# Due times of the first batch's value loads, sums of squares and scale in an attention and feed-forward kernel

## The chip, the cores and the metric

The kernel runs as one program on one NeuronCore of a Trainium2 chip. Its five engines are named as in the profile: PE (matrix products), DVE (vector), ACT (activations), POOL and SP, the last of which here only issues transfers. The metric is device time in microseconds (us) of one execution; lower is better. A time before is the median of three executions.

## The reference, cut to what matters

Four batches of 576 tokens and 8 heads of width 64 pass through causal attention with a decay, then through two gated feed-forward blocks of width 512.

```
scores = scale * q @ k.T + (cum[:, None] - cum[None, :])   # cum: running sum of log f, causal mask
attn   = softmax(scores)
x      = attn @ v                                          # per head, heads joined to 512
h = relu(x @ w_in);  u, vv = halves(h);  vn = layernorm(vv)
x = (u * (w_spatial @ vn + b)) @ w_out
x = sigmoid(xr @ w_r) * (relu(xk @ w_k)**2 @ w_v)          # xk, xr: mixes of x and x shifted by a token
```

## The kernel before

Attention is worked in 16 pairs of heads (`p`), 32 heads in all (`g`); batch `b` is pairs 4b to 4b+3. For each pair the kernel loads q and k, squares and sums them to choose a power of two as their scale (`qksq`, `qkscale`), splits them into a high and a low half (`qkhi`, `qklo`), turns them around by a transposing transfer (`qklo` issues it), copies parts of the result into second tiles (`kaux`, `qaux`), computes scores (`score`, L302) and row maxima (`rowmax`, L311 on DVE), and sends the maxima through memory back into a tile (`mrow`). Only then come the transposed scores (`scoreT`, L335), the exponential (L339), and the product with the values (`pv`, L357). Meanwhile the first feed-forward weight is loaded in eight blocks (`wload`, L90), converted (`wconv`), summed (`wscale`) and split (`wsplit`, L440 on ACT and L441 on DVE).

The values of batch 0 are loaded by `vload` in five chunks `c` of two transfers each, all on SP's queue: ten transfers, eight of 128 KB and the two of the last chunk of 64 KB. `vsq` squares each chunk on ACT and sums it into a column of `va`. `vscale` adds the columns up with two small products on PE and turns the sum into a scale by six short DVE instructions (L234, L78, L79, L81, L85, L238). The scale is first read by `recip` of pair 0, due at 2.4; the values are first read by `pv` of head 0, due at 1.0.

```python
    for e in range(2):                                     # vload
        self.nc.sync.dma_start(t[:tn, c, :, 128 * e:128 * e + 64], src[e::2, t0:t0 + tn]...)
    self.sumsq(self.va[:, c:c + 1], t, self.junka...)      # vsq, L66 on ACT
```

**The order.** Each step is entered with a due time, in units of a head, and a priority; `run` sorts by due time, then priority, and emits the steps in that order. The due times that matter here, from the table `P` and the loops (pair `p` adds 2p): the transposing transfers of pair 0 are issued at -4.25 (k) and -3.95 (q), its copies at -3.6 and -3.5; the values of batch 0 are loaded at -3.2, squared at -3.0 to -1.8, and scaled at -1.2; pair 1 is transposed at -2.25 and -1.95 and copied at -1.6 and -1.5; pair 3's k and q are loaded at -2.0 and -1.7; pair 2 is squared at -1.6 and -1.5 and its scale follows at -1.2; `wsplit` of the first four weight blocks stands at -1.4 to -0.5; pair 4's load is at 0.0 and weight block 4's at 0.15.

**The list behind the order.** The emitted order is not the order on the chip. The program is built with `schedule_with_timeline_sim=True` (L869): the framework walks through the emitted program on a timeline of its own and, whenever an engine's queue is free there, appends the earliest emitted instruction that is ready. So a step emitted later goes ahead where an earlier one still waits. Instructions that pass through `pin` (L56) stay behind the instruction emitted before them on the same engine; `wconv` and `wsplit` use it. On the chip each queue then runs as written.

Of the kernel before, what the change touches and what calls it, by code (L numbers as in the profile page):

```python
# [30 lines left out]
P = dict(load=-8.0, sq=-5.6, ss=-5.2, sc=-5.0, hik=-4.6, lok=-4.25, hiq=-4.2, loq=-3.95, aux=-3.6,  # L31
         s=-2.4, m=-0.65, t=0.0, pv=1.0, out=1.35, rc=1.4, nr=1.9, xs=2.2, xl=2.4, mlp=2.7, mlplen=7.0, vload=-5.0, vsq=-3.0,
         w1=-3.8, w0=1.0, wsp=4.6)
# [6 lines left out]
class K:  # L40
# [561 lines left out]
    def add(self, t, prio, fn, *args):  # L602
        self.steps.append((t, prio, len(self.steps), fn, args))
# [7 lines left out]
    def plan_attention(self):  # L611
        add, G = self.add, self.B * self.H
        for p in range(G // 2):
            T = 2.0 * p
            if p > 1:
                add(T + P["load"], 9, self.load, p, "k")
                add(T + P["load"] + 0.3, 9, self.load, p, "q")
            for i, nm in enumerate("kq"):
                add(T + P["sq"] + 0.1 * i, 2, self.qksq, p, nm)
            add(T + P["ss"], 2, self.qkscale, p)  # L620
            add(T + P["hik"], 2, self.qkhi, p, "k", "act")
            add(T - 4.2, 2, self.crow, p)
            add(T + P["lok"], 2, self.qklo, p, "k")
            add(T + P["hiq"], 2, self.qkhi, p, "q", "dve")
            add(T + P["loq"], 2, self.qklo, p, "q")
            add(T + P["aux"], 2, self.kaux, p)
            add(T + P["aux"] + 0.1, 2, self.qaux, p)
            for h in range(2):
                for u in range(4):
                    add(T + P["s"] + h + 0.22 * u, 4, self.score, 2 * p + h, u)  # L630
                    add(T + P["s"] + h + 0.22 * u + 0.05, 1, self.rowmax, 2 * p + h, u)
            add(T + P["m"], 0, self.mrow, p)
        for g in range(G):
            for u in range(4):
                add(g + P["t"] + 0.22 * u, 0, self.scoreT, g, u)
            for c, u in ((0, 0), (1, 1), (2, 2), (3, 2), (4, 3)):
                add(g + P["t"] + 0.22 * u + 0.06, 1, self.causal, g, c)
            for hf in range(2):
                add(g + P["pv"] + 0.3 * hf, 5, self.pv, g, hf)
            add(g + P["out"], 1, self.head, g)  # L640
            if g % 2:
                add(g + P["rc"], 1, self.recip, g // 2)
                add(g + P["nr"], 2, self.norm, g // 2)
                add(g + P["xs"], 2, self.xhi, g // 2)
                add(g + P["xl"], 2, self.xlo, g // 2)
        for b in range(self.B):
            for c in range(5):
                add(8 * b + P["vload"] + 0.2 * c if b else -3.2, 9, self.vload, b, c)
                add(8 * b + P["vsq"] + 0.3 * c, 3, self.vsq, b, c)
            add(8 * b + P["vsq"] + 1.8, 3, self.vscale, b)  # L650

# [219 lines left out]
```

## Time and profile before

| | us |
|---|---|
| median of three executions | 751.83 (749.38 to 755.04) |
| the profiled execution | 752.66 |
| its span, first to last instruction | 750.9 |

Busy shares of the span are PE 90%, DVE 57%, ACT 50%, POOL 25%. The span falls into a filling stage of about 60 us in which the first pairs are loaded and prepared, an attention stage to about 444 us in which attention and the first feed-forward block share PE, and a last stage of matrix products. In a row of the timeline the first number is the start in us from the span's first instruction and the second the duration; what stands in brackets at the end is the engine's idle time before it and what ended it. SPq rows are the issuing of transfers on SP's queue, not their landing.

### The profile page before, as it was taken

The numbers are of one execution on the slowest core, as the hardware profiler recorded it, in microseconds if no ns is written. First come the engines' busy times: TensorE is split into PE (matmuls) and PEld (weight loads), VectorE is DVE, ScalarE is ACT, GpSimd is POOL, SyncE is SP. The second block draws the span as 40 slices with busy tenths as digits, with TensorE's granted clock in tenths as the row PEclk, the third lists the DMA queues.
The fourth block names the chain that finished last, engine by engine and source line by source line (L and its number), as shares of the span: only waits on it lengthen the run. The fifth ranks groups of instructions, "written<-read, shape, count | busy, mean of one in ns | idle before, by whom it ended". The sixth has DMA issues, their size and how long they took to land.

```text
span 750.9 us, 11016 instructions
## 1 busy us (share of the span) xinstructions
PE 674.9 (90%) x3718; PEld 499.5 (67%) x3718; DVE 426.8 (57%) x1147; ACT 372.2 (50%) x740; POOL 184.5 (25%) x385
## 2 busy tenths in 40 slices
PE   0377878989998999999997679999999999999997
PEld 0245545647775677666774458788888888888886
DVE  5987786666655656646026879988225512632342
ACT  4626786666426854355505539747225412622431
POOL 7122645555324544445321201000000000000000
PEclk9998968999999999999999899999999999999999
DMA  9997666765655234410025453450100100010010
GB/s 228 203 204 158 168 138 131 147 137 107 126 133 122 56 71 99 97 27 18 18 64 184 146 192 124 140 164 15 42 27 16 57 0 15 1 56 1 1 57 28
DMA packets 130681, 69.78 MB, mean 93 GB/s; under 512 B 114704, under 2 KB 115312, under 8 KB 130624
## 3 DMA queue, kind: packets, MB, share of 16 engines
q1 hardware_dynamic: 128032, 67.89, 37.1%
q10 hardware_dynamic: 2592, 1.19, 0.7%
q8 instruction: 29, 0.48, 0.3%
q14 instruction: 28, 0.23, 0.1%
HBM read 42.06 MB, written 9.79 MB: 69 GB/s over the span
## 4 chain that ended last, share of the span: by engine, by line
PE 60%; DMA 16%; DVE 10%; POOL 5%; issue 3%; ACT 3%; SPq 1%; DVEq 0%; ACTq 0%; POOLq 0%
PE m L715 40%; PE o L357 7%; DMA sr<-rd 3%; POOL x L388 3%; PE m L575 3%; PE m1v L504 3%; PE s L302 3%; PE t L335 2%; PE m1u L558 2%; DMA rd<-r 2%; DVE junk L311 2%; DMA r<-rd 2%; DMA wst<-in_moe_w_k_dram 1%; DMA rd<-xo 1%; DMA wst<-in_moe_w_in_dram 1%
## 5 line engine op out<-in xcount | busy, mean ns | idle before, releaser
L357 PE MATMUL o<-e,v 128*128 128x320 f32 (+4 forms) x448 | 114.0, 384 | 5.5 <-POOL e L344 3.7
L715 PE MATMUL m<-xx,moe_w_k 128*128 128x512 f32 (+1 forms) x480 | 107.5, 373 | 0.4 <-ACT x L710 0.4
L715 PE MATMUL m<-moe_w_v,k 128*128 128x512 f32 x432 | 104.8, 391 | 0.0
L339 ACT ACTIVATE e<-t,qa 128x512 f32<-128x512 f32 (+1 forms) x128 | 72.6, 590 | 50.4 <-PE t L335 50.1
L311 DVE CUSTOM_DVE_ANT_0 junk<-s,mask 128x512 bf16<-128x512 f32 (+4 forms) x160 | 75.9, 474 | 37.8 <-PE s L302 32.2
L715 PEld LDWEIGHTS m<-xx,moe_w_k 128*128 128x128 f32 x480 | 84.0, 188 | 18.1 <-ACT x L710 0.9
L357 PEld LDWEIGHTS o<-e,v 128*128 128x128 f32 x448 | 78.5, 199 | 23.7 <-POOL e L344 6.1
L715 PEld LDWEIGHTS m<-moe_w_v,k 128*128 128x128 f32 x432 | 80.7, 188 | 17.7
L344 POOL TENSOR_SCALAR_AFFINE_SELECT e<-e 128x128 f32<-128x128 f32 (+1 forms) x160 | 52.2, 342 | 125.5 <-ACT e L339 123.0
L751 DVE TENSOR_TENSOR tmp<-tmp 128x512 f32<-128x512 f32 (+1 forms) x40 | 25.5, 638 | 88.1 <-ACT tmp L750 87.9
L302 PE MATMUL s<-kT,qT 128*128 128x512 f16 (+2 forms) x192 | 55.8, 299 | 21.6 <-DVE nm L311 13.7
L504 PE MATMUL m1v<-win,xt 128*128 128x512 f16 x240 | 61.5, 397 | 0.0
L388 POOL TENSOR_TENSOR x<-xo,sr 64x576 f32<-64x576 f32 x32 | 47.0, 1469 | 47.6 <-DMA sr<-rd 46.4
L715 PE MATMUL m<-gh,moe_w_out 128*128 128x512 f32 (+1 forms) x240 | 55.1, 380 | 3.5 <-DVE u L578 3.5
L335 PE MATMUL t<-qA,kA 69*128 69x512 f16 (+2 forms) x192 | 51.6, 294 | 7.3 <-DMA qA<-md 6.7
L558 PE MATMUL m1u<-xt,win 128*128 128x288 f16 x384 | 53.6, 286 | 4.5 <-ACT u L560 4.5
L750 ACT ACTIVATE tmp<-m 128x512 f32<-128x512 f32 (+1 forms) x40 | 22.1, 556 | 71.6 <-PE m L715 71.4
L575 PE MATMUL m<-wspT,vn 128*128 128x288 f16 x384 | 54.4, 290 | 3.0 <-DVE u L578 2.3
L302 PE MATMUL s<-kA,qA 67*128 67x512 f16 (+2 forms) x192 | 50.6, 300 | 4.0 <-DMA kA<-kT 3.7
L701 POOL COPY x<-x 128x4 f32<-128x4 f32 x4 | 3.5, 884 | 198.1 <-ACT x L710 198.1
L715 PEld LDWEIGHTS m<-gh,moe_w_out 128*128 128x128 f32 x240 | 43.3, 193 | 13.0 <-DVE u L578 3.8
L335 PE MATMUL t<-qT,kT 128*128 128x512 f16 (+2 forms) x192 | 51.4, 293 | 0.0
(159 smaller groups left out, 1083.8 us busy)
## 6 DMA issues: line engine op xcount, KB each, us to landing
sr<-rd SPq DMA_DIRECT2D x32, 144.0 KB
gd<-u SPq DMA_DIRECT2D x16, 288.0 KB
out_dram<-o SPq DMA_DIRECT2D x18, 256.0 KB
knat<-in_k_dram SPq DMA_DIRECT2D x32, 128.0 KB
v<-in_v_dram SPq DMA_DIRECT2D x32, 128.0 KB
g<-gd SPq DMA_DIRECT2D x16, 256.0 KB
wst<-in_moe_w_k_dram SPq DMA_DIRECT2D x8, 512.0 KB
wst<-in_moe_w_v_dram SPq DMA_DIRECT2D x8, 512.0 KB
```

Source lines behind the costliest of these rows:

```text
L302: self.nc.tensor.matmul(s[:, o:o + n], self.tok(qn, p, h, 128 * ib - 64, 128)[0:r], self.tok(kn, p, h, k0, n)[0:r], start=(j == 0), stop=( ...
L311: self.nc.vector.tensor_tensor_reduce(out=self.junk[r0:, 0:n], in0=self.s[u % 2][r0:, o:o + n], in1=self.mask[r0:, m0:m0 + n], op0=ALU.add ...
L335: self.nc.tensor.matmul(t[:, o:o + n], self.tok(kn, p, h, 128 * c, 128)[0:r], self.tok(qn, p, h, q0, n)[0:r], start=(j == 0), stop=(j == 1))
L339: self.nc.scalar.activation(self.e[g][:, 512 * u:512 * u + n], t[:, 0:n], AF.Exp, scale=self.qa[p][:, 5:6])
L344: self.nc.gpsimd.affine_select(out=e, in_=e, pattern=[[1, n]], compare_op=ALU.is_ge, fill=0.0, base=0, channel_multiplier=-1)
L357: self.nc.tensor.matmul(o[:, 256 + f:256 + q1], v[:, c, h // 2, 64 * (h % 2):64 * (h % 2) + 128], e[:, off:off + q1 - f], start=(c == 0), ...
L388: self.nc.gpsimd.tensor_tensor(self.xp[r], self.xo[h][r], self.sr[r], ALU.mult)
L504: nc.tensor.matmul(self.m1p, xt[:, xs, 128 * j:128 * j + 128], self.win[:, ws, kc, 512:1024], start=(kc == 0 and n == 0), stop=(kc == 3 an ...
L558: self.nc.tensor.matmul(o, self.win[:, ws, kc, fs], self.xt[(4 * b + kc) % 8][:, xs, ts_], start=(kc == 0 and n == 0), stop=(kc == 3 and n ...
L575: nc.tensor.matmul(o, pairs[n][0], pairs[n][1], start=(n == 0), stop=(n == 13))
L715: self.nc.tensor.matmul(out, l, r, start=(first and j == 0), stop=(last and j == len(pairs) - 1))
L751: nc.vector.tensor_tensor(tmp[:, 0:n], tmp[:, 0:n], tmp[:, 0:n], ALU.mult)
```

## The change

The first batch's three kinds of steps get later due times. The ten value loads go from -3.2 to between -1.5 and -0.7, the five squarings from -3.0...-1.8 to -1.2...0.0, the scale from -1.2 to 0.6. Other batches keep theirs. No instruction is added, removed or given another size. In the emitted program the value loads now stand behind pair 1's transposes and copies and behind pair 3's loads, the squarings behind pair 2's, and the scale behind pair 2's and behind the first head's first transposed scores.

```diff
         for b in range(self.B):
+            vsq = 8 * b + P["vsq"] if b else -1.2
             for c in range(5):
-                add(8 * b + P["vload"] + 0.2 * c if b else -3.2, 9, self.vload, b, c)
-                add(8 * b + P["vsq"] + 0.3 * c, 3, self.vsq, b, c)
-            add(8 * b + P["vsq"] + 1.8, 3, self.vscale, b)
+                add(8 * b + P["vload"] + 0.2 * c if b else -1.5, 9, self.vload, b, c)
+                add(vsq + 0.3 * c, 3, self.vsq, b, c)
+            add(vsq + 1.8, 3, self.vscale, b)
```

## Rows read from the trace of the kernel before

**Rows 1.** The page's busy tenths in 40 slices of 18.8 us.
```profile
PE   0377878989998999999997679999999999999997
DMA  9997666765655234410025453450100100010010
```

**Rows 2.** Stretches: length; busy us of PE, PEld, DVE, ACT, POOL; clock; DMA; GB/s.
```profile
0.00:28.00 28.00, 2.10 (x6) 1.22 (x7) 18.48 (x36) 13.03 (x28) 15.37 (x43) 1.00 1.02 225
28.00:41.00 13.00, 7.00 (x30) 4.06 (x31) 12.12 (x47) 8.43 (x19) 1.56 (x1) 1.00 0.99 201
41.00:60.00 19.00, 17.25 (x87) 10.30 (x85) 16.77 (x59) 8.57 (x16) 7.65 (x19) 1.00 0.89 191
60.00:145.00 85.00, 72.19 (x389) 47.35 (x389) 61.60 (x231) 57.38 (x124) 41.32 (x73) 0.84 0.70 146
145.00:200.00 55.00, 51.30 (x343) 34.48 (x342) 36.54 (x119) 34.84 (x76) 26.99 (x57) 0.97 0.58 124
```

**Rows 3.** Chain that ended last, 9 to 62 us: start, us, what.
```profile
21.39 4.66 DMA wst<-in_moe_w_in_dram
...
34.20 0.07 DVE va L234
```

**Rows 4.** Timeline of SP's queue, 13 to 33 us: start, us, transfer issued.
```profile
13.62 3.28 SPq L222 DMA_DIRECT2D v<-in_v_dram  x6
17.03 0.42 SPq L206 DMA_DIRECT2D cumd<-u  x1
17.49 0.43 SPq L222 DMA_DIRECT2D v<-in_v_dram  x1
18.02 1.56 SPq L272 DMA_TRANSPOSE qT<-nq  x1
...
23.38 0.49 SPq L278 DMA_DIRECT2D kA<-kT  x1
23.93 2.02 SPq L222 DMA_DIRECT2D v<-in_v_dram  x3
26.00 1.64 SPq L272 DMA_TRANSPOSE kT<-nk  x1
27.68 1.15 SPq L215 DMA_DIRECT2D knat<-in_k_dram  x2
...
29.54 1.42 SPq L272 DMA_TRANSPOSE qT<-nq  x1
31.01 1.25 SPq L215 DMA_DIRECT2D qnat<-in_q_dram  x2
```

**Rows 5.** Timeline of PE at the first scores.
```profile
28.01 0.96 PE L302 MATMUL s<-kA,qA 67*128 67x512 f16 x2 [3.69 <-DMA kA<-kT]
```

**Rows 6.** Timeline of ACT, 17 to 46 us.
```profile
17.65 0.63 ACT L66 ACTIVATE junka<-v 128x512 bf16<-128x512 f32 x1 [0.45 <-DMA v<-in_v_dram]
...
28.39 0.63 ACT L66 ACTIVATE junka<-v 128x512 bf16<-128x512 f32 x1 [1.67 <-DMA v<-in_v_dram]
...
29.02 0.61 ACT L66 ACTIVATE win<-wf 128x512 f16<-128x512 f32 x1
...
30.37 0.74 ACT L66 ACTIVATE junka<-knat 128x640 bf16<-128x640 f32 x1
...
32.45 1.95 ACT L440 ACTIVATE win<-wf,sw 128x512 f16<-128x512 f32 x3 [0.39 <-DVE sw L81]
...
45.02 0.83 ACT L260 ACTIVATE nk<-knat,qa 128x640 f16<-128x640 f32 x1 [7.07 <-DVE qa L81]
```

**Rows 7.** Timeline of DVE, 26 to 42 us.
```profile
26.07 1.27 DVE L100 TENSOR_SCALAR wst<-wst 128x512 int32<-128x512 int32 x1 [0.33 <-DMA wst<-in_moe_w_in_dram]
...
33.46 0.74 DVE L441 SCALAR_TENSOR_TENSOR win<-wf,sw,win 128x512 f16<-128x512 f32 x1
...
41.09 0.15 DVE L238 TENSOR_SCALAR sv<-sv 128x1 f32<-128x1 f32 x1
41.16 0.17 DVE L318 CAST nmh<-nm 128x10 f16<-128x10 f32 x1
```

## The prediction

> **What bounds the kernel now.** I read the page's slices first: PE is busy for nine tenths or more in most of them, but 0, 3 and 7 tenths in the first three, while DMA stands at nine tenths in just these [rows 1]. So the change falls into the filling stage, the one place where PE is not the bound. Next the busy time by stretch: to 28 us PE works 2.1 us; from 28 to 41 us DVE is busy 12.12 of 13 us and PE only 7.0; from 41 to 60 us PE has 17.25 of 19 [rows 2]. The DMA engines are full to 41 us at 201 to 225 GB/s. Then the chain of waits: a weight block's landing at 26.05 us starts DVE's conversions, and from there the chain runs through DVE almost without a break to about 41 us [rows 3]. Then the four queues that the change touches, each in order of time [rows 4 to 7]. A microsecond saved before 41 us can move the end only if it comes off one of two things: the landing that opens the first scores at 28.01 us [rows 5], or DVE's queue between 28 and 41.16 us, where the last row maximum of pair 0 lets `mrow` start [rows 7].
>
> **The change part by part.**
>
> *The value loads on SP.* The list appends what is ready. In the trace the first six loads are issued in one run from 13.62 us, and `cumd`, which was emitted long before them, only behind that run; the seventh follows at 17.49 us [rows 4]. So the list put them there because nothing emitted earlier was ready. What the new due time lets pass ahead of them is pair 1's transposes and copies and pair 3's loads. The first need pair 1's split halves; pair 3's loads go into pair 0's tiles and need pair 0's halves done, which is also what pair 0's transposes, issued from 18.02 us behind the seventh load, waited for. None was ready, so I expect seven of ten to stay where they are: 0 us. The other three (128 and twice 64 KB, 256 KB) come at 23.93 us, behind pair 0's copy `kA<-kT`. There pair 3's k load is ready (emitted at -2.0, before the values' -1.5), and the two change places: k's three transfers, 288 KB, for 256 KB in front of pair 1's k transpose. At 201 GB/s the 32 KB are 0.16 us, on a transpose whose result the first pair does not read. Then q of pair 3 takes the place that k had, and the three value loads land on q's old place: from 23.93 on, k takes 1.86 us (27.68 to the next row's 29.54), q as long, the two transposes 1.64 and 1.42, 6.8 us together, so they go out at about 31 us [rows 4].
>
> Does anything urgent get faster by that? `kA<-kT` was issued at 23.38 us and ended PE's wait at 28.01 [rows 5]; chunk 3, whose second transfer was issued right behind it, ended ACT's wait at 28.39 [rows 6]. They landed in the order of issue, so taking away the later one gives the earlier one 0. If the engines shared their time among both, 256 KB at 201 GB/s would give up to 1.27 us. I take 0, the order in the rows, and keep -1.27 as a bound. The Trainium skill, DMA: Bandwidth & Descriptors, section Queues, rings and completion order, states that each DMA engine consumes descriptors in ring order though completions need not follow it; by that the gain is 0 too, and the rule speaks against the idea that what is asked for later frees what stands ahead. By equal sharing it would be the 1.27.
>
> *The squarings on ACT.* Five of 0.63 us and five read-outs of the sum. They were fillers: the first waited 0.45 us for its data, the fourth 1.67 [rows 6]. Pair 2's squarings (0.74 us each) now stand earlier in the program and should take the first fillers' places at about 17.2 us; in the trace they ran only at 30.37, behind all the values' [rows 6]. The weight's last squaring at 29.02 us stood behind the fourth filler, which ran from 28.39: at most 0.12 us gained, if I set its input's arrival at about 28.9. Where the fillers go: ACT was idle for 7.07 us before 45.02 [rows 6], so their five places cost 0. If that cover is gone they cost 5 x 0.63 = 3.2 us, but of ACT, which is busy 8.57 of 19 us from 41 to 60 [rows 2].
>
> *The scale.* Two small products on PE: no cost, PE is half idle from 28 to 41 us [rows 2]. Six short DVE instructions now stand inside the DVE-bound stretch; the last runs at 41.09, directly before `mrow`'s first at 41.16 [rows 7], and the chain gives one of them 0.07 us net [rows 3], the spacing of those two rows. Six are 0.4 us. With the squarings of the last two chunks waiting for loads of about 31 us they should pass behind 41.16. Pair 2's five scale instructions go the other way, ahead of 26 us: 5 x 0.07 = 0.35 us out of the stretch, into one where DVE waited 0.33 us for the weight block anyway [rows 7], so they cost 0.02 there. Bounds: 0 if the list puts all eleven back between the row maxima; 11 x 0.15 = 1.65 us if the full duration counts.
>
> **The sum.** 0 (loads) - 0.12 (ACT) - 0.4 - 0.33 (DVE) = -0.85 us. Behind 60 us PE has the say, so a start 0.85 earlier is an end at most 0.85 earlier. The profiled execution took 752.66, so 751.8; it lies 0.83 above the median of 751.83, so against the runs shown I predict **751.0**.
>
> **Rivals.**
>
> *A, the loads do go behind.* If the list did not fill the gap at 13.62 us, seven loads (896 KB at 225 GB/s, 4.0 us) would leave the queue ahead of pair 0's transposes, the weight block would land about 4 us before 26.05 and `kA<-kT` before 28.01. Both of the chain's starts would gain about 4 us: 747.8. For it speaks only the wording of the due times; against it that `cumd`, emitted first, was overtaken by six loads.
>
> *B, a new wait on ACT (slower).* Where the list puts chunk 3's and 4's squarings ahead of the three `wsplit` products at 32.45 us, ACT waits for loads issued at about 31 us. They took 4.46 us before (23.93 to 28.39), so they end at 35.5; the weight's DVE part moves from 33.46 by 3 us, and the row maxima behind it in DVE's queue with it. +3 us against the profiled execution, 755.7; against the median 754.8. It decides from the point at which the list's own timeline lets these loads land before `wsplit`'s scale is ready. For it: the list already misjudged these loads by 1.67 us at 28.39 [rows 6]. Against it: `wsplit` is emitted ahead of them and needs only chunks 0 to 2 by its pins. The Trainium skill, TensorE: Matmul & The Clock Gate, in its table of specifications calls ACT's and DVE's queues strict first in, first out; the row at 28.39, with the weight's squaring behind it, agrees. The same price holds if pair 2's halves, ready sooner, make DVE wait for pair 1's transposes.
>
> *C, the list falls differently later.* Every order behind the first difference can change. From 60 to 145 us PE is idle 12.8 of 85 us (15%), from 145 to 200 us 3.7 of 55 (7%), with clocks of 0.84 and 0.97 [rows 2]. If the first stretch ran with the second's share of idle time it would gain 85 x 0.083 = 7.1 us: 744.7; as much lost is 758.9. Nothing in the rows favours one sign.
>
> **How the numbers follow.** The forecast has 0.50, A 0.10, B 0.18, C 0.12 faster and 0.10 slower. About 1% (7.5 us) is what a measurement of this kernel can tell from no change; forecast, A and B lie inside it, and C reaches its edge on either side. Half of C and a tenth of A and B may pass it, and C's faster side a little more, as DVE loses work there: faster by over 1% 0.12, within 1% 0.77, slower 0.11. The forecast's own range is 749 to 752, from its bounds (-2.9 with sharing and full durations, +0.2 with nothing gained). To leave out no more than 2 in 10 the range must hold A, B and most of C: 744 to 759.
>
> **What would show it.** Right: six value loads still from about 13.6 us and one behind `cumd`; three at about 31 us; pair 2's squarings on ACT before 20 us; `mrow` at 40.3 instead of 41.16. Wrong by A: transposes of pair 0 before any value load, and first scores near 24 us. Wrong by B: an idle gap on ACT ended by `v` ahead of L440. Wrong by C: the first 60 us alike and PE's idle time from 60 to 145 us changed by over 4 us.

## The result and the profile after

The changed kernel takes 755.88 us (median of 20 executions, 750.27 to 760.68) against 751.71 us (20, 747.72 to 755.04) for the kernel before on the same chip: a ratio of 1.0055 with an interval of 1.0035 to 1.0075. It is slower by some 4 us. The profiled execution of the changed kernel is the fastest of its twenty (750.27 us, span 748.6 us, mean granted clock 0.982), so its trace shows the order well, but not where the loss lies. For that a second trace of the same order is used (e1 below, span 761.3 us, clock 0.961). Traces of one order differ from execution to execution; where a reading hangs on one trace, the others of its order are named with it.

SP's queue after, in order of time (start, us, transfer issued); it answers to [rows 4]:

```profile
13.96 3.34 SPq L222 DMA_DIRECT2D v<-in_v_dram  x6
...
17.89 0.43 SPq L222 DMA_DIRECT2D v<-in_v_dram  x1
...
24.52 1.22 SPq L215 DMA_DIRECT2D knat<-in_k_dram  x2
...
33.79 1.97 SPq L222 DMA_DIRECT2D v<-in_v_dram  x3
...
42.02 0.66 SPq L90 DMA_DIRECT2D wst<-in_moe_w_in_dram  x1
...
43.81 0.38 SPq L325 DMA_DIRECT2D md<-mr  x1
...
46.91 0.22 SPq L326 DMA_DIRECT2D qA<-md  x1
```

The same queue before, where [rows 4] end:

```profile
36.75 0.59 SPq L90 DMA_DIRECT2D wst<-in_moe_w_in_dram  x1
...
43.58 0.31 SPq L325 DMA_DIRECT2D md<-mr  x1
...
45.35 0.39 SPq L326 DMA_DIRECT2D qA<-md  x1
```

Seven of the ten value loads still go out at 13.96 and 17.89 us, three at 33.79. New is the row at 42.02: weight block 4 (512 KB), which before went out at 36.75, now stands 1.8 us ahead of the first row-max reload, `md<-mr` and `qA<-md`.

ACT after, in order of time; it answers to [rows 6]. An idle time stands in brackets with what ended it:

```profile
16.83 0.73 ACT L66 ACTIVATE junka<-knat 128x640 bf16<-128x640 f32 x1
...
29.41 0.63 ACT L66 ACTIVATE win<-wf 128x512 f16<-128x512 f32 x1 [2.26 <-DVE wf L105]
...
32.98 1.95 ACT L440 ACTIVATE win<-wf,sw 128x512 f16<-128x512 f32 x3 [2.85 <-DVE sw L81]
...
37.64 0.63 ACT L66 ACTIVATE junka<-v 128x512 bf16<-128x512 f32 x1 [0.55 <-DMA v<-in_v_dram]
```

Pair 2's squarings run at 16.83 us instead of 30.37. The wait ahead of L440 was ended by DVE's scale, not by a value load.

DVE after; it answers to [rows 7]:

```profile
26.49 1.36 DVE L100 TENSOR_SCALAR wst<-wst 128x512 int32<-128x512 int32 x1
...
32.16 0.15 DVE L78 TENSOR_SCALAR qa<-tot 128x2 f32<-128x2 f32 x1
...
41.33 0.18 DVE L318 CAST nmh<-nm 128x10 f16<-128x10 f32 x1
...
45.52 0.15 DVE L238 TENSOR_SCALAR sv<-sv 128x1 f32<-128x1 f32 x1
```

The values' scale left the stretch (its last instruction is at 45.52, behind the cast at 41.33). Pair 2's scale did not (its first at 32.16).

PE after at the first transposed scores, and the chain of waits of the same trace just ahead of it:

```profile
50.62 0.59 PE L335 MATMUL t<-qA,kA 69*128 69x512 f16 x1 [2.24 <-DMA qA<-md]
```

```profile
43.81 3.08 DMA md<-mr
46.89 0.02 issue
46.91 3.67 DMA qA<-md
```

Two transfers of 5 KB took 3.08 and 3.67 us. PE waited 2.24 us for them and started L335 at 50.62. Before, it did so at 47.36, without a wait:

```profile
47.36 0.63 PE L335 MATMUL t<-qA,kA 69*128 69x512 f16 x1
```

Busy times by stretch in e1, the changed order again (length; busy us of PE, PEld, DVE, ACT, POOL; clock; DMA; GB/s):

```profile
41.00:60.00 19.00, 15.70 (x81) 9.49 (x81) 14.24 (x62) 6.56 (x13) 5.60 (x17) 1.00 0.96 224
60.00:145.00 85.00, 66.91 (x359) 43.78 (x357) 60.98 (x226) 55.97 (x123) 37.13 (x63) 0.84 0.68 138
```

The stretch from 60 to 145 us in the changed kernel's own trace:

```profile
60.00:145.00 85.00, 69.72 (x395) 45.26 (x394) 65.59 (x241) 60.35 (x130) 41.80 (x74) 0.90 0.70 148
```

Against [rows 2], PE works 5.3 us less in e1 from 60 to 145 us, at the same clock of 0.84, and 2.5 us less in the changed kernel's own trace, at 0.90. That is the stretch to look at.

### The profile page after: what moved, and what is told of

It is laid out like the page before. It is cut to its first block, busy times and chain, and to the rows that moved or that the text cites. A ratio compares the mean times of both kernels' runs of the same rounds, so it can differ in the third digit from the quotient of the medians.

```text
span 748.6 us, 11020 instructions
## 1 busy us (share of the span) xinstructions
PE 669.3 (89%) x3718; PEld 496.4 (66%) x3718; DVE 425.2 (57%) x1147; ACT 372.1 (50%) x740; POOL 180.6 (24%) x385
## 3 DMA queue, kind: packets, MB, share of 16 engines
q1 hardware_dynamic: 128032, 67.89, 36.7%
## 4 chain that ended last, share of the span: by engine, by line
PE 51%; DMA 17%; DVE 14%; POOL 5%; ACT 5%; issue 4%; SPq 3%; DVEq 0%; ACTq 0%; POOLq 0%
PE m L716 37%; PE o L357 4%; PE m L575 4%; DMA sr<-rd 3%; POOL x L388 3%; DVE junk L311 2%; PE t L335 2%; DMA r<-rd 2%; DMA rd<-r 2%; PE s L302 2%; DMA gd<-u 1%; DMA qA<-md 1%; DMA rd<-xo 1%; DMA knat<-in_k_dram 1%; PE m1u L558 1%
## 5 line engine op out<-in xcount | busy, mean ns | idle before, releaser
L344 POOL TENSOR_SCALAR_AFFINE_SELECT e<-e 128x128 f32<-128x128 f32 (+1 forms) x160 | 46.8, 310 | 124.2 <-ACT e L339 122.2
L335 PE MATMUL t<-qA,kA 69*128 69x512 f16 (+2 forms) x192 | 50.2, 286 | 9.7 <-DMA qA<-md 6.9
L504 PE MATMUL m1v<-win,xt 128*128 128x512 f16 x240 | 57.3, 379 | 0.0
L558 PE MATMUL m1u<-xt,win 128*128 128x288 f16 x384 | 53.6, 286 | 4.0 <-ACT u L560 4.0
L302 PE MATMUL s<-kA,qA 67*128 67x512 f16 (+2 forms) x192 | 51.1, 303 | 3.5 <-DMA kA<-kT 3.2
L716 PE MATMUL m<-moe_w_r,xx 128*128 128x512 f32 x216 | 50.3, 392 | 0.0
L335 PE MATMUL t<-qT,kT 128*128 128x512 f16 (+2 forms) x192 | 50.2, 286 | 0.0
```

Source lines behind the costliest of these rows:

```text
L302: self.nc.tensor.matmul(s[:, o:o + n], self.tok(qn, p, h, 128 * ib - 64, 128)[0:r], self.tok(kn, p, h, k0, n)[0:r], start=(j == 0), stop=( ...
L335: self.nc.tensor.matmul(t[:, o:o + n], self.tok(kn, p, h, 128 * c, 128)[0:r], self.tok(qn, p, h, q0, n)[0:r], start=(j == 0), stop=(j == 1))
L344: self.nc.gpsimd.affine_select(out=e, in_=e, pattern=[[1, n]], compare_op=ALU.is_ge, fill=0.0, base=0, channel_multiplier=-1)
L504: nc.tensor.matmul(self.m1p, xt[:, xs, 128 * j:128 * j + 128], self.win[:, ws, kc, 512:1024], start=(kc == 0 and n == 0), stop=(kc == 3 an ...
L558: self.nc.tensor.matmul(o, self.win[:, ws, kc, fs], self.xt[(4 * b + kc) % 8][:, xs, ts_], start=(kc == 0 and n == 0), stop=(kc == 3 and n ...
L716: self.nc.tensor.matmul(out, l, r, start=(first and j == 0), stop=(last and j == len(pairs) - 1))
```

## The experiments

**How they are made.** Each kernel below computes everything. A function at the end of the program's body writes every engine's order down and chains each instruction to the one ahead of it on its engine, so that the list can't reorder what is not meant to move:

```diff
     for p in (k.ps3, k.p2, wst, k.p3, wp, k.hl, k.c):
         p.release()
+    hold(tc)      # each engine's order as written in ORDER
```

Where two orders are joined "at t", the instructions up to t stand in the one kernel's relative order and all others in the other's. In the diffs `load6 k` is the issue of pair 6's k load, `md1` and `qA1` are the two transfers of pair 1's row-max reload (L325, L326), and so on. All ratios are to the kernel before on the same chip. The table gives by how many us the k-th matrix product, counted from 0, starts later than in the trace of before (which has them at 51.1, 69.8, 99.5, 135.6, 233.9, 322.4 and 746.7 us); the orders differ, so it is progress, not the same product.

| kernel | ratio (interval) | 75th | 150th | 300th | 450th | 1050th | 1650th | last |
|---|---|---|---|---|---|---|---|---|
| changed, own trace | 1.0055 (1.0035–1.0075) | +3.9 | +0.7 | +2.6 | -0.1 | -4.2 | -1.2 | -2.4 |
| e1 | 1.0106 (1.0075–1.0137) | +2.9 | +3.2 | +7.2 | +4.8 | +1.2 | +12.3 | +10.3 |
| e4 | 0.9992 (0.9971–1.0013) | +2.3 | -0.4 | -1.8 | -0.4 | -2.5 | -1.2 | +3.1 |
| e5 | 1.0084 (1.0059–1.0109) | +0.1 | +3.3 | +7.9 | +5.0 | +1.2 | +6.8 | +8.3 |
| e7 | 1.0087 (1.0056–1.0118) | +2.5 | +3.2 | +7.7 | +6.6 | +4.2 | +6.3 | +6.1 |
| e8 | 1.0041 (1.0015–1.0068) | +0.7 | +1.1 | 0.0 | +0.4 | -2.6 | +3.0 | +6.6 |
| e9 | 1.0094 (1.0064–1.0124) | +2.9 | -0.2 | +6.3 | +3.8 | +0.2 | +4.1 | +6.5 |
| e10 | 1.0040 (1.0017–1.0064) | +0.1 | +4.8 | +3.3 | +3.6 | +1.7 | +2.9 | +5.4 |
| e17 | 1.0074 (1.0043–1.0105) | +2.5 | +1.5 | +7.3 | +4.9 | +1.7 | +6.2 | +7.2 |
| e18 | 1.0099 (1.0063–1.0136) | +0.8 | +3.0 | +10.7 | +9.1 | +9.5 | +9.5 | +10.0 |

Traces of one order spread: in e4, whose order behind 62 us is that of before, the progress moves by up to 3 us either way, and the first two rows, one order in two measurements, lie 4.6 us apart at the 300th product and 12.7 at the last. So a few us at the end are for the ratios, and a wait of a single trace is read only against the other traces of its order.

**e1: the changed order, held.** No edit but the hold. It is the changed kernel measured a second time, with the kernel before beside it.

> The changed kernel with the order of every engine's instructions written down and held, nothing else altered: a control for the method, and a second trace of the changed kernel. Queue theory and later-order theory both expect the changed kernel's 755.9 us (ratio to before about 1.0055), first exponential near 51.7 us.

The medians are 762.33 us against 753.73 and the ratio is 1.0106, with its interval just touching that of the first measurement (1.0035 to 1.0075). Every engine's instructions stand in the same order in both traces. So the ratio itself moves by up to half a per cent from one measurement to another, and ratios from different chips that differ by less are not told apart below.

### The start

**e2 and e3: weight blocks 4 and 5.** In e2 the changed order has them moved up, in e3 the order of before has them put where the changed kernel has them:

```diff
 e2:  values 0 (last three)
+     wload 4
      ... pair 2's transposes
-     wload 4
      ... md0 ...
-     wload 5
      qA0
+     wload 5
 e3:  the same moves the other way, in the order of before
```

> The changed kernel's order held, with two transfers moved on SP's queue alone: weight block 4's load from ahead of pair 0's row-maxima store to ahead of pair 4's k load, and weight block 5's load from ahead of the row maxima's reload to behind it. Queue theory (the row maxima of pair 0 stand behind two blocks of 512 KB, 1.3 us at the store and 1.7 us at the reload): first exponential about 3 us earlier, near 48.7 us, and the end with it, about 753 us, ratio 1.001. Later-order theory (the loss is made behind 65 us by the other order of the list): first exponential earlier too, but the end stays at about 756.

> The kernel before with its order held, and weight blocks 4 and 5 put on SP's queue where the changed kernel has them: block 4 between pair 2's transposes and the row-maxima store, block 5 ahead of the reload. Nothing else differs from before. Queue theory: first exponential near 51.3 instead of 48.45 us and about 754.7 us, ratio 1.004. Later-order theory: the start is later but the end is 751.7, ratio 1.000.

e2 brought the first exponential from 51.04 us (e1) to 49.06 and measured 1.0077 (1.0048 to 1.0107), not told apart from e1. e3 put the delay into the kernel before: first exponential 50.98 instead of 48.45, 75th product at 53.6 instead of 51.1. By the 150th product it had vanished (70.1 against 69.8), and the ratio is 1.0001 (0.9982 to 1.0020). So the late first exponential comes from the place of these two transfers, and no cost of it shows.

**e4 and e5: whose start, whose rest.** e4 is the changed order to about 62 us and that of before behind; e5 the reverse.

> A mixed order: the first 400 dispatches (to about 62 us) in the order of the changed kernel, all behind them in the order of the kernel before. Queue theory: as late as the changed kernel, about 755, ratio 1.004. Later-order theory: the start costs nothing, 751.7, ratio 1.000.

> A mixed order: the first 400 dispatches (to about 62 us) as in the kernel before, all behind them as in the changed kernel. The reverse of the mix with the changed start. Later-order theory: as slow as the changed kernel, ratio 1.0055 to 1.010, although its first exponential comes near 48.5 us. Queue theory (the loss is made in the first 62 us): ratio 1.000.

0.9992 (0.9971 to 1.0013) and 1.0084 (1.0059 to 1.0109). The whole stretch that the change was made for costs and brings nothing beyond 0.3%; the loss arises in what follows, with instructions that the diff doesn't name. Over the whole execution it isn't a lower clock either: e5's twelve executions have a mean granted clock of 0.971, as have the 24 of the kernel before beside them.

### Where behind 62 us

**e6, e7, e8 and e12: the join moved.** Changed order to 120 us (e6) and to 206 us (e7), then that of before; order of before to 206 us (e8) and to 275 us (e12), then the changed one.

> The first 920 dispatches (to about 120 us) in the changed kernel's order, the rest in the order of the kernel before. If the loss is made between 62 and 120 us: ratio 1.005 to 1.01. If it is made later: 1.000.

> The first 1800 dispatches (to about 206 us, the point where the two orders lie closest) in the changed kernel's order, the rest as before. If the loss is made between 120 and 206 us, where the two orders lie farthest apart: ratio 1.005 to 1.01. If it is made behind 206 us: 1.000.

> The first 1800 dispatches as before, the rest (206 to about 325 us, behind which the two orders are the same) in the changed kernel's order. If the loss is made behind 206 us, as the second trace of the changed kernel suggests (11 us lost between matmul 1050 and 1650): ratio 1.005 to 1.01. If it is made ahead of that: 1.000.

> The order of the kernel before up to about 275 us, then that of the changed kernel. The order of before up to 206 us and the changed one behind gave 1.0041. If that remainder arises between 206 and 275 us, this run is at 1.000 within its interval; if it arises behind 275 us, where the two orders still differ up to about 325 us, it stays near 1.004.

1.0142 (1.0108 to 1.0176), 1.0087 (1.0056 to 1.0118), 1.0041 (1.0015 to 1.0068) and 1.0053 (1.0027 to 1.0079). e7 has the changed order only to 206 us and costs as much as e5, on the same chip, which has it from 62 us to its end: unless its join costs something, the stretch from 62 to 206 us is enough for the loss. e8 and e12 also cost something, with the changed order behind 206 and 275 us alone (the two orders are the same from about 311 us on, but for a few of DVE's conversions up to 442). But e6 costs more than the whole changed order, so a join can cost something of its own, and whether e8 and e12 pay for the late order or for their join is not shown.

Within the stretch the traces place it. From the 150th to the 300th product, about 70 to 107 us, the order of before takes 28.3 to 30.1 us in seven traces (before, e3, e4, e8, e12, e15, e16) and the changed order 31.7 to 34.3 in six (its own, e1, e2, e5, e6, e7). PE is idle 2.7 to 4.7 us of it in the first and 5.3 to 6.7 in the second, at mean granted clocks of 0.86 to 0.99 and 0.82 to 0.93. From the 300th to the 450th the changed order takes 33.2 to 34.9 us against 36.0 to 37.5 (without e6, whose join lies there), so it gives a part back.

### What waits between 62 and 106 us

SP's queue around pair 1's reload in the trace of before:

```profile
57.04 0.38 SPq L325 DMA_DIRECT2D md<-mr  x1
57.46 2.15 SPq L222 DMA_DIRECT2D v<-in_v_dram  x4
59.72 0.54 SPq L90 DMA_DIRECT2D wst<-in_moe_w_in_dram  x1
...
62.58 0.83 SPq L326 DMA_DIRECT2D qA<-md  x1
```

And in e1:

```profile
58.93 0.38 SPq L325 DMA_DIRECT2D md<-mr  x1
...
60.74 1.10 SPq L215 DMA_DIRECT2D knat<-in_k_dram  x2
61.89 0.61 SPq L216 DMA_DIRECT2D knat<-in_k_dram  x1
62.54 0.59 SPq L215 DMA_DIRECT2D qnat<-in_q_dram  x1
...
64.94 0.55 SPq L90 DMA_DIRECT2D wst<-in_moe_w_in_dram  x1
65.54 0.29 SPq L326 DMA_DIRECT2D qA<-md  x1
```

In the changed order pair 6's loads stand ahead of weight block 7 and of the reload (before they follow at 71.19); why the list put them there is not shown. PE at that place in the trace of before, in e1 and in the changed kernel's own trace:

```profile
66.26 0.58 PE L335 MATMUL t<-qA,kA 69*128 69x512 f16 x1 [2.55 <-DMA qA<-md]
```

```profile
69.56 0.61 PE L335 MATMUL t<-qA,kA 69*128 69x512 f16 x1 [4.20 <-DMA qA<-md]
```

```profile
68.23 0.39 PE L335 MATMUL t<-qA,kA 69*128 69x512 f16 x1 [1.03 <-DMA qA<-md]
```

4.20 us against 2.55 looks like the cause, but 1.03 us belongs to the changed order too. This wait is 0.85 to 4.67 us in the seven traces that have the order of before here (before, e3, e4, e8, e12, e16, e18) and 1.03 to 5.27 in the six of the changed order. So no pair of these traces shows what the loads cost; e9 and e10 move them.

**e9 and e10: the loads behind, the loads ahead.**

```diff
 e9 (changed order)                 e10 (order of before)
  md1, values 4                      md1, values 2 to 4
- load6 k k k q                     +load6 k k k q
  transpose k3, wload 7, qA1         wload 7, row 0, transpose k3, qA1
  ... copies of pair 3               ... copies of pair 3
+ load6 k k k q                     -load6 k k k q
  (load7 q q likewise, behind        (load7 q q likewise, ahead of md2)
   pair 4's copies)
```

> The changed kernel with every engine's order held; on SP's queue alone, pair 6's three k transfers and first q transfer go from ahead of pair 3's k transpose, weight block 7 and pair 1's row-max reload to behind pair 3's copies, and pair 7's first two q transfers to behind pair 4's copies, where the kernel before has such loads. If these loads, which become ready earlier in the changed order, delay pair 1's and pair 2's reload (later order, SP's part), PE's wait ahead of pair 1's transposed scores falls from 4.2 us to about 2.5, the 150th matrix product comes about 2 to 3 us earlier than the 73.0 us of the held order, and the ratio to before falls from 1.0106 to about 1.006. If the loss of 60 to 120 us lies in the order of PE, ACT or DVE and not in this queue, the 300th product stays about 7 us behind the kernel before and the ratio at 1.010.

> The kernel before with every engine's order held; on SP's queue alone, pair 6's three k transfers and first q transfer are put ahead of weight block 7 and pair 1's row-max reload, and pair 7's first two q transfers ahead of pair 2's reload, as the changed kernel has them. If the place of these loads is what costs, weight block 7 and the reload go out some 2 to 3 us later, the 150th product comes 2 to 3 us later than 69.8 us, and the ratio is 1.003 to 1.006. If it is not, the delay is taken up as the delay of the first exponential was, and the ratio stays within 0.002 of 1.

PE in e9, and in e10, at pair 1's transposed scores:

```profile
66.67 0.39 PE L335 MATMUL t<-qA,kA 69*128 69x512 f16 x1 [1.02 <-DMA qA<-md]
```

```profile
71.08 0.59 PE L335 MATMUL t<-qA,kA 69*128 69x512 f16 x1 [6.29 <-DMA qA<-md]
```

e10: the wait was 6.29 us, longer than in any trace above, and the end moved, 1.0040 (1.0017 to 1.0064, one measurement). Unlike the late start, a delay at these places was not taken up; which of the delayed transfers carries it, weight block 7, the transposes or the reloads, was not separated. e9: the wait was 1.02 us and the 150th product level with before, as expected, but by the 300th it was 6.3 us late again, and the ratio of 1.0094 (1.0064 to 1.0124) can't be told from e1's. So the place of these loads is enough to lose time, and moving them back doesn't win back what the changed order loses.

**e11: the scale's products first.** In e1 DVE waited 3.93 us for the small products of weight half 0 and pair 4, which now stood behind head 2's value products on PE. This wait does tell the orders apart: 2.0 to 4.8 us in the six traces of the changed order, 0.3 to 1.6 in the seven with the order of before.

```diff
 e9's order, on PE:  value product 1 of head 2
+                    wscale 0, qkscale 4
                     ... value product 3 of head 2
-                    wscale 0, qkscale 4
```

> As the changed kernel with the loads behind the reloads, and on PE's queue the three small products for the second weight half's and pair 4's scale go from behind the fifth value product of head 3's predecessor to directly behind the first value product of head 2, next to where the kernel before has them. In the held order DVE waited 3.93 us for them and everything behind them on DVE (pair 4's split, the row maxima) was late. If that wait is the second half of the loss, the 300th product comes within 2 us of the kernel before's 99.5 us and the ratio falls to about 1.002 to 1.004 (the part behind 206 us remains); if it only moves the wait, the ratio stays that of the run with the loads moved alone.

The wait fell to 1.10 us, and yet the ratio is 1.0108 (1.0063 to 1.0153) and the 300th product 7.1 us late: nothing gained.

**e15: the reload still earlier in the kernel before.**

```diff
 order of before:  md1, values
+                  qA1
                   wload 7, row 0, transpose k3
-                  qA1
```

> The kernel before, held, with one transfer moved on SP's queue: pair 1's row-max reload goes ahead of weight block 7, head 0's row and pair 3's k transpose. If this reload's place sets the end, PE's 2.5 us wait ahead of pair 1's transposed scores shrinks by 1.5 to 2.5 us and the ratio falls to about 0.997 to 0.998; if a gain at this place is given back later, the 150th product is early by as much and the ratio stays within 0.001 of 1.

PE no longer waits for this transfer (1.51 us for an exponential take its place), the 150th product comes 1.3 us earlier, and the ratio is 0.9986 (0.9966 to 1.0006): a gain of 0.1%, which is not told apart from none.

**e17 and e18: two more groups of transfers.** e9's POOL and ACT rows show two further queue heads that wait:

```profile
77.61 3.21 POOL L388 TENSOR_TENSOR x<-xo,sr 64x576 f32<-64x576 f32 x2 [3.36 <-DMA sr<-rd]
```

```profile
97.11 0.68 ACT L66 ACTIVATE junka<-ws 128x576 bf16<-128x576 f32 x1 [3.06 <-DMA ws<-in_moe_w_spatial_dram]
```

The masks of the next head stand behind the first, exponentials behind the second. Neither wait marks the changed order as such: ACT's is at most 0.77 us in its six traces and 1.07 in that of before, POOL's 0 to 2.47 us against 0.42. e17 takes these waits away in the changed order, e18 puts them into the order of before:

```diff
 e17 (e9's order)                       e18 (order of before)
  copies of pair 3                       values 4
+ recip 0 (back), load6 mixed in        +load6 k k k
  load6 ...                              recip 0 (back)
- recip 0 (back)                        -load6 k k k
  copies of pair 4                       copies of pair 4
+ spatial weights, biases               -spatial weights, biases
  load7 q q, recip 1                     row 3, load7 k k k, recip 1
- spatial weights, biases               +spatial weights, biases
```

> The changed kernel, held, with three groups of transfers ahead of the later pairs' loads on SP's queue: pair 1's row-max reload (as in e9), the two transfers that bring back pair 0's reciprocals, and the spatial weights and biases. In e9 POOL's norm waited 3.4 us for the second group with the masks of the next head queued behind it, and ACT's squaring of a spatial weight 3.1 us for the third with exponentials behind it. If these waits at the heads of POOL's and ACT's queues are the second half of the loss, both shrink by about 2 us, the 300th product comes 3 us or more earlier than e9's 105.8 us, and the ratio falls from e9's 1.0094 to 1.003 to 1.006. If the loss is spread over the changed order's many small waits, the 300th stays at 105 or more and the ratio at 1.008 or more.

> The reverse in the kernel before, held: on SP's queue pair 6's k loads go ahead of pair 0's reciprocals, and pair 7's k loads and pair 1's first reciprocal transfer ahead of the spatial weights and biases, which go out some 4 us later; the row-max reload stays. If late transfers of this kind cost, POOL's and ACT's waits grow by 2 to 4 us, the 300th product comes 2 us or more late and the ratio is 1.003 or more; if they are taken up, it stays within 0.002 of 1.

In e18, ACT and then PE:

```profile
99.55 0.68 ACT L66 ACTIVATE junka<-ws 128x576 bf16<-128x576 f32 x1 [3.81 <-DMA ws<-in_moe_w_spatial_dram]
```

```profile
101.00 3.75 PE L357 MATMUL o<-e,v 128*128 128x256 f32 x8 [3.32 <-ACT xo L365]
```

ACT's wait grew from 1.07 us to 3.81, PE waited 3.32 us behind it, the 300th product came 10.7 us late and the ratio is 1.0099 (1.0063 to 1.0136), all the way to the end. Two groups of transfers later in one queue (the reciprocals from 70.80 to 74.12 us, the spatial weights from 83.00 to 93.81) cost about as much as the whole change. In this trace PE's wait for pair 1's reload was also long (4.67 us), though its place was left alone, so not all of the 10 us belong to the two; and the granted clock was lower, 0.968 in the mean against 0.972 of the kernel before beside it. In e17 ACT's wait for the spatial weights is gone and POOL's for the reciprocals is 0.98 us, yet the 300th product stays 7.3 us late and the ratio, 1.0074 (1.0043 to 1.0105), is not told apart from e1's. DVE still waited 3.97 us for PE's products. From the 150th to the 300th product e9, e11 and e17 take 35.5 to 36.7 us, with PE idle for 6.3 to 7.9: more than the changed order as it stands. Where one wait was taken away, others took its place.

**e13, e14 and e16: one queue of the other order.** SP's whole order from 54 to 206 us exchanged, the other four engines left: e13 the changed kernel with SP as before (as near as the other orders allow), e14 the reverse; e16 as e14, behind 206 us.

```diff
 e13:  PE, ACT, DVE, POOL of the changed kernel
-      SP of the changed kernel
+      SP of the kernel before, 54 to 206 us
 e14, e16:  the reverse, 54 to 206 us and behind 206 us
```

> The changed kernel with the order of PE, ACT, DVE and POOL held as it is, and SP's queue alone, from about 54 to 206 us, put back into the order of the kernel before as far as the other engines' orders allow. If the loss up to 206 us comes from SP's order (what is queued ahead of the row-max reload, the reciprocals' transfers and the spatial weights), the 300th matrix product comes within 3 us of the kernel before's 99.5 us and the ratio falls from 1.0106 to 1.002 to 1.005, the rest being what arises behind 206 us. If it comes from the other four orders, the 300th stays 6 to 7 us behind and the ratio at 1.008 or more.

> The reverse: the kernel before with its own order on PE, ACT, DVE and POOL, and SP's queue from about 54 to 206 us in the changed kernel's order. If SP's order is the cause, the 300th product comes 4 us or more late and the ratio is 1.005 or more (moving pair 6's and 7's loads alone gave 1.0040); if the four other orders are, the ratio stays within 0.003 of 1.

> The kernel before with its own order on the four engines, and SP's queue behind 206 us in the changed kernel's order (32 places differ). If SP's order is also what costs behind 206 us, the ratio is near the 1.0041 and 1.0053 of the two kernels that run the changed order from 206 and 275 us on; if that remainder is the other engines' order, the ratio is 1.000 within its interval.

1.0519 (1.0486 to 1.0553), 1.0270 (1.0225 to 1.0315) and 1.0028 (0.9998 to 1.0057). PE's waits in e14, 60 to 200 us (us in total, times, longest), then in e13:

```profile
PE t L335 <- DMA qA<-md: 18.4, 4, 8.8
```

```profile
PE o L357 <- POOL e L344: 20.5, 4, 10.7
```

In the trace of before the first of these comes to 4.9 us in 3 times. Either mixture is far slower than both whole orders. So the question that e13 and e14 were meant for, SP or the others, has no answer of this kind: here a queue's order went only with the other four. e16 can't be told from 1, nor from e8.

## Why the prediction was wrong

**The mechanism forecast was there in part, and it did not matter.** The value loads did as said: seven stayed, the six in one run. The last three came at 33.79 us, not 31, because pair 1's copies, which I had named among what goes ahead, were left out of the 6.8 us (32.14 to 33.74), and the queue ran some 0.6 us late. The first scores gained nothing, as the value chosen had it: from the issue of `kA<-kT` to the first product that reads it the ten traces with the changed start take 4.54 us in the mean, the ten with the start of before 4.51.

**The gain of 0.85 us shrank to about 0.3.** `mrow`'s cast came at 41.33 us instead of 41.16. The conversion that opens the stretch came 0.42 us later (26.49 against 26.07), so the stretch itself is 0.25 us shorter; over ten traces with either start it is 14.75 us in the mean against 15.08 (14.46 to 14.93 and 14.79 to 15.21). The 0.4 for the values' scale is there, in that its six instructions left the stretch; but other rows of DVE moved by as much, such as L270 (1.42 us at 37.58 before, 0.87 after) and the first L441 (1.03 us at 34.52 after, 0.74 before), so the 0.3 isn't theirs alone. The 0.33 for pair 2's scale is not there: its squarings moved to 16.83 us, but the products on PE that add them up ran only at 31.18, and DVE took the scale at 32.16, inside the stretch. ACT's 0.12 is not there either, since its last weight squaring waited for DVE (29.41).

**A moved transfer was overlooked.** The steps had no term for weight block 4. It had been issued at 36.75 us and now went out behind pair 2's transposes, at 42.02, right ahead of the first reload; the first exponential came at 51.67 instead of 48.45 us. That is a worse start, where I had forecast a better one.

**The step that failed: from the start to the end.** "Behind 60 us PE has the say, so a start 0.85 earlier is an end at most 0.85 earlier" takes the rest of the program as given. e3 shows that a start 2.5 us later is taken up within 20 us, and e4 that the whole changed start costs nothing; in the other direction, e5 shows that the changed rest costs 0.84% behind an unchanged start. The end was set by the order that the list chose for what comes later, which the diff doesn't touch. That is rival C on its slower side, to which I gave 0.10; the range of 744 to 759 us holds the 755.88 only by the room left for it. Its sign in the text came in part: from 60 to 145 us PE works 5.3 us less in e1, more than the 4 us named there, but 2.5 less in the changed kernel's own trace, and the first 60 us were not alike. Its price, 7.1 us, lies between the 4 us of the first measurement and the 8.6 of e1, but by luck: it was worked out as a gain, from the idle share of another stretch, and turned around.

**Rival B did not come.** ACT's wait ahead of L440 was ended by DVE, and the last value squarings ran behind it with a wait of 0.55 us. **Rival A did not come**: six value loads from 13.96 us.

**What is shown of C, and what stays open.** Shown: the loss lies behind 62 us (e4, e5), and, unless e7's join costs something, the stretch from 62 to 206 us is enough for it. In the traces it opens between the 150th and the 300th product, by more idle time of PE and a lower clock. Shown too: loads and transfers put later on SP's queue lose 0.4 to 1.0% in the kernel before (e10, e18). Not shown: that the changed order loses its time by these. It has pair 6's loads in the place that cost in e10, but the waits at the reload and at the spatial weights lie in the same range in its traces as in those of before. Taking single waits away did not bring the time back (e9, e11, e17), and exchanging a whole queue made its own waits (e13, e14). Whether it is one further wait or the sum of many small ones, and whether the changed order costs anything behind 206 us (e8, e12), is not settled.

## What to carry to other kernels

Where a framework orders the program by a list, a change of due times in one corner is a new order everywhere behind it: price it as a redraw of the whole order, with the spread of that, and not as the sum of the steps that move. To tell the two apart, hold each engine's order, join the old and the new one at a few points, and see which part carries the time; join both ways, since a join can cost something itself (e6). Before a wait is called the cause, look for it in other traces of the same order. Ask of every transfer on a shared queue what stands behind its reader: here a late one was free in the start (e3) and cost 0.4 and 1.0% where masks, exponentials or scores stood behind the waiting instruction (e10, e18), while an earlier one gained nothing (e15).

## What the runs showed of the hardware

- **Behind a wait PE can run at its lower clock for some us.** At pair 1's reload the granted clock fell to 0.50, the lower of its two levels (1.2 and not 2.4 GHz), during the waits of 2.55 (before), 4.20 (e1) and 6.29 us (e10), and stayed there for some 7 us; the product of 512 columns behind the wait took 0.58, 0.61 and 0.59 us. In e9 and in the changed kernel's own trace, behind 1.02 and 1.03 us, it took 0.39 at the full clock. The length of the wait doesn't decide it alone: the same product took 0.39 behind 2.65 us in e2 and 0.58 behind 1.02 in e12, and in e9 the clock fell 1.6 us after it all the same. Nor is every slow product the granted clock's: the row at 47.36 took 0.63 us while the granted clock was 1.00 [rows 2].
- **DVE's split of a weight block slows down while POOL works.** In the trace of before, L441 took 0.74 us with POOL idle (33.46 us [rows 7]; POOL next works at 36.77) and 1.79 us beside POOL's products of two tiles. Where L441 was first and a mask on POOL began beside it, it took 0.75, and the mask 0.59 instead of the 0.29 of the same mask at 69.31 us:

```profile
74.52 0.75 DVE L441 SCALAR_TENSOR_TENSOR win<-wf,sw,win 128x512 f16<-128x512 f32 x1
...
75.99 1.79 DVE L441 SCALAR_TENSOR_TENSOR win<-wf,sw,win 128x512 f16<-128x512 f32 x1
```

```profile
69.31 0.29 POOL L344 TENSOR_SCALAR_AFFINE_SELECT e<-e 128x128 f32<-128x128 f32 x1 [0.89 <-ACT e L339]
...
74.83 0.59 POOL L344 TENSOR_SCALAR_AFFINE_SELECT e<-e 128x128 f32<-128x128 f32 x1 [2.57 <-ACT e L339]
75.84 3.22 POOL L388 TENSOR_TENSOR x<-xo,sr 64x576 f32<-64x576 f32 x2 [0.42 <-DMA sr<-rd]
```

  So when a transfer that POOL waits for lands also decides which DVE instructions run beside POOL. The Trainium skill, SBUF — State Buffer, section Who interferes with whom, says that a DVE instruction with two inputs in SBUF contends with a GpSimd instruction that reads there; these rows agree.
- **A small transfer took longer with a large one ahead of it on its queue.** The reload's first 5 KB took 3.08 us with 512 KB asked for 1.8 us ahead of it; in the trace of before, with no such block there, it was issued at 43.58 us and its second step, which waits for it, at 45.35, so it took at most 1.77. From the first step's issue to the second's, nine traces with the blocks as in the changed order show 3.1 to 3.7 us and nine with them as before 1.8 to 2.4; moving blocks 4 and 5 alone gave 2.2 in e2 and 2.8 in e3.
